# First rows' f32 products of the first two dense steps issued per tile of 128 rows, and a new table of places

## The chip, the core and the metric

The kernel runs on one core of one Trainium2 chip. The metric is device time in microseconds (us) of one execution, from the program's start to its end on that core; less is better.

## What is computed

Attention with a memory branch, and behind it a two-layer network on all 2304 rows:

```
scores = q @ k.T / 8, causal;  a = softmax(scores);  local = a @ v          # per batch and head, S=576, D=64
mem    = (phi(q) @ M_prev) / (phi(q) . z_prev + 1e-6)                        # phi(x) = elu(x) + 1
attn   = g * mem + (1 - g) * local                                           # g = sigmoid(beta) per head
x      = attn as [2304, 512]                                                 # 4 batches x 576 rows, 8 heads x 64
h      = x @ w_in                                                            # [512, 2048]
y      = (max(h, 0) + alpha * min(h, 0)) @ w_out                             # [2048, 512]
```

The two weights arrive as 64-bit floats; VectorE turns them into f32 with integer operations (three instructions for a piece of 128 rows).

## The kernel before

**Rows.** A batch has 576 rows: 64 first rows and four tiles of 128. The first 64 rows of the four batches make one group of 256 rows, called Z in the code (`gz`, batch number 4 in names), in two tiles of 128 rows, t = 0 and 1. Each other group has two tiles of 128 rows of one batch.

**First rows.** For each tile of Z the kernel turns q and k with TensorE (`tZ0`, `tZ1`), makes scores (`sZ0`, `sZ1`, PSUM tiles `s_0_69` and `s_0_68`, row maxima `zmx`), exponentials on ScalarE, and probabilities beside the memory branch's factors in the tiles `P_99` and `P_100` (`p4`, `oZ0`, `oZ1`). TensorE turns these and multiplies with the values; ScalarE writes the result in f32 to `x32` (`R` in the trace), 128 columns per tile. The scaling of the values needs their largest magnitude (`v4`), which needs the last of the loads of the first rows' v and M_prev.

**Dense steps.** The network goes in steps j = 0 to 7 of 256 of the 2048 hidden columns. For Z (and for the first group of batch 0) steps 0 to 3 are done in f32 straight from the converted weights `R`; step j of Z has phase name `h4_10j`. Before, such a step is two accumulation groups (f = 0, 1) of four matmuls with 256 moving columns, both tiles of rows at once, into one of two PSUM tiles (`h_126`, `h_125`); then ScalarE's relu into `r`, and two VectorE instructions into `gg`. Later steps use f16 halves of weights and rows, three matmuls where f32 has one. The second product (`y4_10j` and so on) accumulates in two PSUM tiles `y`, which are also used for turning.

**Order.** Nothing is scheduled while the program runs. Every instruction is recorded with a phase name; the table `PLACES` gives each instruction of each phase its place, and the program is written out in the order of these numbers. An engine runs its own instructions strictly in that order, so that one that waits holds up all behind it; DMAs are issued in that order too, almost all from SyncE's queue (SP in the trace).

```
places = {k: iter(map(int, x.split())) for k, x in PLACES.items()}
at = [next(places[op[7]]) for op in self.ops]
for i in sorted(range(len(at)), key=at.__getitem__):
```

**Fillers.** 40 f16 matmuls of `ones` (phases `N`, `n`) into `h_125` compute nothing that is used; they stand at the start of TensorE's order between the first rows' short pieces of work. Eight f32 matmuls `h_125<-R` (phases `n0` to `n3`) are fillers too.

**Names.** `C0x`, `D0x` and `C1x` are VectorE's conversions of the first half of the weights (outputs `R`), `C2x` and `C3x` those of the second half; `ast`, `oma` and `scd` come from alpha, which TensorE turns first (`bank<-ident,xn`); `bk0x` and `BK0x` turn q and k of batch 0, `s0..` are its scores, `P0..` its probabilities, `o0..` its values; `q1`, `bk1x` prepare batch 1. Nearly every instruction has line L1748, the line that writes out the recorded program, so tiles tell them apart.

Of the kernel before, what the change touches and what calls it, by code (L numbers as in the profile page):

```python
# [32 lines left out]
    "LZ0": (  # L33
        "28"
    ),
    "LZ1": (
        "35"
    ),
    "Lz": (
        "29 34 0"  # L40
    ),
    "LK0": (
        "89"
    ),
    "LK1": (
        "86"
    ),
    "LV0": (
        "96 95"
    ),  # L50
    "LV1": (
        "178 179"
    ),
    "I": (
        "1 7 2 8 9 31 10"
    ),
    "z": (
        "37 32 38 44 33 90"
    ),
    "N": (  # L60
        "6 11 12 13 14 15 16 17 18 19 20 21 22 23 24 25"
    ),
    "n": (
        "40 41 42 58 59 78 85 87 102 130 134 135 136 137 138 139 140 141 142 143 192 193 194 195"
    ),
    "J": (
        "43 49 50 51 175 39 53 54 55 56 61 64 69 70 72 75 80 77"
    ),
    "a4": (
        "66 98 100 116 117 167"  # L70
    ),
    "K": (
        "5 26"
    ),
    "tZ0": (
        "45 46 47 48 81 91 92 93 94 103 105"
    ),
    "sZ0": (
        "60 104 106 107 108 109 110 111 112 113 114 115 118 119 120 121 122 123 126 165 212 145 185 164 166 215 186"
    ),  # L80
    "tZ1": (
        "82 83 84 88 124 127 128 129 131 132 147"
    ),
    "sZ1": (
        "146 148 149 150 151 152 153 154 155 156 157 158 159 160 161 162 163 182 187 223 226 225 188 227 213 189 224"
    ),
    "v4": (
        "133 180 184 197 198 201 203 204 654 205"
    ),
    "p40": (  # L90
        "65 67 68 73 74"
    ),
    "p41": (
        "79 97 99 101 125"
    ),
    "p4": (
        "168 170 173 181 206 207 214 183 208 217 240"
    ),
    "oZ0": (
        "216 220 221 222 233 234 235 242 236 237 238 239 253 243 244 245 246 247 265 266 267 268 269 270 271 272 275 "  # L100
        "276 281 282"
    ),
    "oZ1": (
        "228 241 248 249 250 251 252 254 255 256 257 260 261 273 274 279 280 284 285 286 287 292 294 295 296 297 298 "
        "299 300 301"
    ),
    "LW00": (
        "27"
    ),
    "LW01": (  # L110
        "62"
    ),
    "LW02": (
        "171"
    ),
    "LW03": (
        "144"
    ),
    "LX00": (
        "288"  # L120
    ),
    "LX01": (
        "262"
    ),
    "LX02": (
        "283"
    ),
    "LX03": (
        "229"
    ),  # L130
    "C00": (
        "36 52 57"
    ),
    "n0": (
        "196 199"
    ),
    "C01": (
        "63 71 76"
    ),
    "n1": (  # L140
        "202 209"
    ),
    "C02": (
        "172 174 176"
    ),
    "n2": (
        "210 211"
    ),
    "C03": (
        "169 177 200"  # L150
    ),
    "n3": (
        "218 219"
    ),
    "D00": (
        "289 290 291"
    ),
    "c0": (
        "328 378 381 382 437 454 525 544 557"
    ),  # L160
    "D01": (
        "277 278 305"
    ),
    "D02": (
        "293 323 368"
    ),
    "D03": (
        "264 321 352"
    ),
    "LW10": (  # L170
        "401 402"
    ),
    "LW11": (
        "395 392"
# [5 lines left out]
        "439 429 466 450 467 468 474 506 529 700 655 656"  # L180
    ),
    "LW12": (
        "451 452"
    ),
    "C11": (
        "398 400 428"
    ),
    "LW13": (
        "446 445"
    ),  # L190
    "C12": (
        "453 455 456"
    ),
    "C13": (
        "447 448 449"
    ),
    "L0q": (
        "315 190 230"
    ),
    "L0k": (  # L200
        "336 332 338 30"
    ),
    "L0v": (
        "469 472 473 464"
    ),
    "a0": (
        "191 258 259 320"
    ),
    "bk00": (
        "306 307 308 309 310 302 303 304 311 329"  # L210
    ),
    "bk01": (
        "347 348 349 356 337 341 342 345 357 358 360 379 346 350 351 359"
    ),
    "v0": (
        "475 476 477 481 484 485 486 489 490 491 1161 492"
    ),
    "p00": (
        "263 313 314 322 366"
    ),  # L220
    "p01": (
        "231 232 312 317 318"
    ),
    "p0": (
        "367 375 383 420 493 494 495 384 496"
    ),
    "L0Q": (
        "316 385"
    ),
    "L0K": (  # L230
        "409 412"
    ),
    "L0V": (
        "509 482"
    ),
    "A0": (
        "319 431 503 520"
    ),
    "BK00": (
        "380 389 394 396 397 387 388 390 391 393"  # L240
    ),
    "BK01": (
        "410 413 416 417 421 411 414 415 418 427"
    ),
    "V0": (
        "510 512 524 580 581 597 612 715 613 679 682"
    ),
    "r02": (
        "425 426 460 540 555"
    ),  # L250
    "r03": (
        "386 399 488 533 554"
    ),
    "r0": (
        "638 647 699 713 714 716 717 712 719"
    ),
    "h4_100": (
        "324 325 326 327 330 331 333 334 335 362 363"
    ),
    "s011": (  # L260
        "440 458 457 459 470 465 500 501 497 498"
    ),
    "P010": (
        "502 504 514 513 532 519 515 526 547 550 551 556 558"
    ),
    "h4_101": (
        "339 340 343 344 353 354 355 361 376 403 377"
    ),
    "y4_100": (
        "434 441 435 442"  # L270
    ),
    "P011": (
        "499 521 517 531 537 527 565 566 567 568 570 571 574"
    ),
    "s013": (
        "507 518 522 534 535 539 528 536 523 553"
    ),
    "P012": (
        "541 542 543 562 589 561 575 588 590 593 594 599 604"
    ),  # L280
    "o011": (
        "601 602 603 621"
    ),
    "P013": (
        "577 578 546 582 538 579 607 608 609 610 622 625 626"
    ),
    "h4_102": (
        "364 365 369 370 371 372 373 374 438 461 462"
    ),
    "y4_101": (  # L290
        "436 443 471 444"
    ),
    "s015": (
        "559 560 563 572 587 591 573 592 576 595"
    ),
    "P014": (
        "614 615 516 616 545 624 627 634 635 636 637 644 645"
    ),
    "o013": (
        "658 659 660 664"  # L300
    ),
    "P015": (
        "628 630 661 631 548 642 663 665 666 667 668 674 675"
    ),
    "s017": (
        "620 639 632 641 652 650 640 653 633 651"
    ),
    "P016": (
        "681 683 606 684 662 691 685 692 693 694 704 705 707"
    ),  # L310
    "h4_103": (
        "404 405 406 407 408 419 423 424 463 479 480"
    ),
    "y4_102": (
        "478 549 487 552"
    ),
    "o015": (
        "676 677 678 697"
    ),
    "P017": (  # L320
        "686 695 605 696 689 706 708 709 710 711 722 723 724"
    ),
    "s031": (
        "738 740 742 739 757 759 761 758 771 766 765 805"
    ),
    "P030": (
        "772 784 781 780 836 878 806 820 1020"
    ),
    "o017": (
        "731 732 733 734"  # L330
    ),
    "bv00": (
        "741 1023 727 730"
    ),
    "bv01": (
        "767 1085 799 807"
    ),
    "bv02": (
        "830 1090 720 721"
    ),  # L340
    "bv03": (
        "810 811 745 796"
    ),
    "P031": (
        "822 842 846 850 847 876 874 875 877"
    ),
    "h0_100": (
        "671 702 718 743 746 747 748 749 752 754 756"
    ),
# [72 lines left out]
    "S22": (
        "839 867"
# [1328 lines left out]
def kernel(  # L1752
# [27 lines left out]
    Z = B  # L1780
    KD = DM // 128
# [57 lines left out]
    def raw(pos):  # L1839
        return R[pos]  # L1840
# [993 lines left out]
```

## Time and profile before

| | |
|---|---|
| three runs | 540.99, 539.5, 540.41 us; median 540.41 |
| profiled execution | 539.77 us, of which the span from first to last instruction is 538.0 |
| TensorE (PE) busy | 524.0 us, 97% of the span |
| VectorE (DVE) busy | 442.0 us, 82% |
| ScalarE (ACT) busy | 390.1 us, 73% |
| GpSimd (POOL) busy | 69.2 us, 13% |
| granted TensorE clock | 1.0 of full speed in every slice |

A busy TensorE is not a TensorE at its peak, since matmuls are pipelined and their ends are modelled; starts are what to go by. Idle time matters only on an engine that others wait for, so each stage has to be asked for itself.

### The profile page before, as it was taken

The page shows a single profiled execution, that of the slowest core. Times are in us where ns is not written, and L with a number is a line of the kernel's source. Part 1 is how long each engine was busy: PE and PEld are TensorE (multiplying, and loading weights), DVE is VectorE, ACT ScalarE, POOL GpSimd, SP SyncE. Part 2 cuts the span into 40 slices and gives each one's busy share as a digit, 9 for nine tenths or more (in the row PEclk, how much of TensorE's full clock was granted, in tenths as well). Part 3 has the DMA queues.
Part 4 walks back from the last instruction along what each step waited for, and adds up shares of the span by engine and source line. Part 5 has one row for each costly group of instructions (what it writes and reads, how often), then busy time and mean ns, then how long its engine had stood idle before and what let it go on. Part 6 is the DMA issues. An engine that isn't in the chain of part 4 may idle for free.

```text
span 538.0 us, 11935 instructions
## 1 busy us (share of the span) xinstructions
PE 524.0 (97%) x4419; PEld 352.6 (66%) x4419; DVE 442.0 (82%) x1167; ACT 390.1 (73%) x820; POOL 69.2 (13%) x142
## 2 busy tenths in 40 slices
PE   9999999999988999999999999999999999999996
PEld 4687456657564767576768666666766667666672
DVE  4999999999999999999987899988478867752321
ACT  4868998779987788988897796876376756842322
POOL 3000310302101021111112120111021110200000
PEclk9999999999999999999999999999999999999999
DMA  9999816669588799668999885659454643641101
GB/s 211 278 283 296 235 61 214 196 191 222 114 158 199 188 213 175 168 148 202 212 168 211 136 148 90 136 131 197 92 105 91 126 95 80 127 104 40 39 1 40
DMA packets 225586, 82.32 MB, mean 153 GB/s; under 512 B 216036, under 2 KB 216052, under 8 KB 225528
## 3 DMA queue, kind: packets, MB, share of 16 engines
q1 hardware_dynamic: 225344, 81.55, 66.4%
q8 instruction: 34, 0.56, 0.4%
q14 instruction: 24, 0.20, 0.1%
q10 hardware_dynamic: 184, 0.02, 0.0%
HBM read 35.15 MB, written 5.77 MB: 76 GB/s over the span
## 4 chain that ended last, share of the span: by engine, by line
PE 79%; DVE 14%; ACT 2%; DMA 2%; issue 1%; DVEq 0%; ACTq 0%
PE h L1748 33%; PE y L1748 32%; PE s L1748 7%; PE bank L1748 6%; DVE R L1748 5%; DMA PT<-P 2%; DVE P L1748 2%; DVE E L1748 2%; DVE q L1748 1%; PE s L1655 1%; DVE gg L1748 1%; DVE r L1748 1%; DVE t L1748 1%; ACT t L1748 1%; ACT R L1748 1%
## 5 line engine op out<-in xcount | busy, mean ns | idle before, releaser
L1748 PE MATMUL y<-R,gg 128*128 128x512 f16 (+1 forms) x832 | 233.6, 396 | 1.4 <-DVE t L1748 1.2
L1748 PE MATMUL h<-x,R 128*128 128x256 f16 x1536 | 214.8, 273 | 0.0
L1748 PEld LDWEIGHTS <-R 128*128 128x128 f16 x1536 | 144.3, 98 | 38.2 <-DVE r L1748 1.5
L1748 PEld LDWEIGHTS <-gg 128*128 128x128 f16 x768 | 72.8, 98 | 60.8 <-issue 2.3
L1748 POOL TENSOR_SCALAR E<-q,nrm,sm 128x64 f32<-128x64 f32 x112 | 56.6, 519 | 333.4 <-DVE sm L1748 246.4
L1748 ACT ACTIVATE E<-E,mx 128x320 f32<-128x320 f32 (+3 forms) x136 | 80.8, 599 | 14.4 <-DVE mx L1748 13.1
L1748 DVE SCALAR_TENSOR_TENSOR P<-E,mx,P 128x640 f16<-128x640 f32 (+3 forms) x112 | 75.8, 701 | 10.4 <-ACT P L1748 10.3
L1748 DVE SCALAR_TENSOR_TENSOR r<-r,oma,h 128x256 f32<-128x256 f32 x128 | 56.9, 472 | 26.3 <-ACT r L1748 26.0
L1748 ACT ACTIVATE P<-E,mx 128x512 f16<-128x512 f32 (+3 forms) x112 | 71.0, 673 | 7.5 <-POOL E L1748 6.2
L1748 PE MATMUL bank<-v,PT 128*128 128x64 f16 x1224 | 75.4, 193 | 1.0 <-DMA PT<-P 1.0
L1748 ACT ACTIVATE r<-h 128x512 f32<-128x512 f32 x72 | 41.8, 589 | 42.3 <-PE h L1748 34.6
L1748 PEld LDWEIGHTS <-PT 128*128 128x128 f16 x1224 | 60.3, 98 | 16.0 <-DMA PT<-P 2.4
L1748 DVE CUSTOM_DVE_ANT_0 E<-s,mask,pm 128x320 f32<-128x320 f32 (+3 forms) x96 | 56.8, 611 | 3.4 <-PE s L1748 2.4
L1748 ACT ACTIVATE gg<-r,gsc 128x512 f16<-128x512 f32 x56 | 39.7, 715 | 26.5 <-PE y L1748 20.1
L1748 DVE SCALAR_TENSOR_TENSOR gg<-r,gsc,gg 128x512 f16<-128x512 f32 x56 | 41.6, 748 | 17.6 <-ACT gg L1748 15.5
L1748 PE MATMUL s<-k,qT 128*128 128x512 f16 (+5 forms) x136 | 36.4, 290 | 1.8 <-DMA qT<-q 1.8
L1748 PE MATMUL s<-k,qS 128*128 128x192 f16 (+4 forms) x120 | 33.8, 294 | 1.2 <-DMA qS<-qT 1.2
L1748 PE MATMUL h<-R 128*128 128x256 f32 x144 | 34.7, 383 | 0.0
L1748 PEld LDWEIGHTS h<-R 128*128 128x128 f32 x144 | 26.1, 190 | 5.3 <-issue 1.7
L1748 ACT ACTIVATE xn<-bank,xsc 128x256 f16<-128x256 f32 x28 | 13.1, 468 | 19.8 <-PE bank L1748 19.7
L1748 ACT ACTIVATION_READ_ACCUMULATOR E<-E,mx 128x1 f32 x124 | 23.3, 188 | 0.0
L1748 ACT ACTIVATE R<-R,wsc 128x1024 f16<-128x1024 f32 x16 | 18.3, 1143 | 5.5 <-DVE R L1748 4.8
(186 smaller groups left out, 611.9 us busy)
## 6 DMA issues: line engine op xcount, KB each, us to landing
q<-in_q_dram SPq DMA_DIRECT2D x18, 256.0 KB, 4.2
vn<-in_v_dram SPq DMA_DIRECT2D x16, 256.0 KB, 4.6
out_dram<-t SPq DMA_DIRECT2D x16, 256.0 KB, 2.3
kn<-in_moe_w_in_dram SPq DMA_DIRECT2D x6, 512.0 KB, 6.0
kn<-in_moe_w_out_dram SPq DMA_DIRECT2D x6, 512.0 KB, 5.2
kn<-in_k_dram SPq DMA_DIRECT2D x12, 256.0 KB, 3.8
qS<-qT SPq DMA_DIRECT2D x24, 128.0 KB, 2.7
R<-in_moe_w_in_dram SPq DMA_DIRECT2D x4, 512.0 KB, 6.5
```

The costliest lines, as they stand in the source:

```text
L1655: first[1](*first[2], **first[3])
L1748: fn(*a, **kw)
```

## The change

Two things change: the code of the first two f32 steps of Z, and the whole table of places. In steps j = 0 and 1 of Z the loop over the two tiles of rows goes outermost: for each tile, each f, the four matmuls with 128 moving columns. That is 16 matmuls of 128 columns where 8 of 256 were, in each of the two steps, and the matmuls of the first tile no longer depend on the second tile's rows. The relu and the two VectorE instructions behind them are unchanged and still wait for all 16. Steps 2 and 3 are unchanged.

```diff
-        for f in range(2):
+        if f32 and g["id"][0] == str(Z) and j < 2:
+            for t in range(2):
+                for f in range(2):
+                    fc = 2 * j + f
+                    for kk in range(KD):
+                        T.matmul(hps[:, f, 128 * t:128 * t + 128], lhsT=raw(kk + 1)[:, fc * 128:fc * 128 + 128],
+                                 rhs=g["x32"][:, kk, 128 * t:128 * t + 128], start=(kk == 0), stop=(kk == KD - 1))
+        for f in range(2) if not (f32 and g["id"][0] == str(Z) and j < 2) else ():
...
     "h4_100": (
-        "324 325 326 327 330 331 333 334 335 362 363"
+        "309 310 311 350 351 355 356 357 358 359 363 365 366 367 368 369 389 418 405"
     ),
...
     "y3_313": (
-        "6213 6214 6215 6220 6221 6222 6216 6217 6218 6223 6224 6225 6219 6226 6230 6049 6228 6229"
+        "6229 6230 6231 6236 6237 6238 6232 6233 6234 6239 6240 6241 6235 6242 6246 6065 6244 6245"
     ),
```

What the new table does to the order is seen at three places.

**At the start.** On TensorE, just behind the two matmuls that spread z_prev (`y<-R`), a filler now stands ahead of the turn of alpha, and one more stands ahead of these matmuls:

```order
 L1748 MATMUL y_124<-R 128x512
 L1748 MATMUL y_123<-R 128x512
+L1748 LDWEIGHTS ones
+L1748 MATMUL h_125<-ones 128x512
 L1748 MATMUL bank_67<-ident,xn_103 128x16
```

So alpha's turn comes two fillers later. On VectorE, from its first conversion on, before:

```order
L1748 TENSOR_SCALAR R<-R 128x512
L1748 TENSOR_SCALAR igc<-igc 128x8
L1748 RECIPROCAL iom<-igc 128x8
L1748 TENSOR_SCALAR iom<-iom 128x8
L1748 SCALAR_TENSOR_TENSOR R<-R 128x512
L1748 TENSOR_SCALAR oma<-bank_67 128x16
L1748 TENSOR_REDUCE ast_89<-bank_67 128x1
L1748 TENSOR_SCALAR ast_89<-ast_89 128x1
L1748 SCALAR_TENSOR_TENSOR R<-R 128x512
L1748 TENSOR_REDUCE scd_87<-bank_67 1x1
```

and now:

```order
L1748 TENSOR_SCALAR R<-R 128x512
L1748 SCALAR_TENSOR_TENSOR R<-R 128x512
L1748 TENSOR_SCALAR igc<-igc 128x8
L1748 SCALAR_TENSOR_TENSOR R<-R 128x512
L1748 RECIPROCAL iom<-igc 128x8
L1748 TENSOR_REDUCE ast_89<-bank_67 128x1
L1748 TENSOR_SCALAR oma<-bank_67 128x16
L1748 TENSOR_SCALAR ast_89<-ast_89 128x1
L1748 TENSOR_SCALAR iom<-iom 128x8
L1748 TENSOR_REDUCE scd_87<-bank_67 1x1
L1748 TENSOR_SCALAR scd_87<-ident,scd_87 1x1
```

The third instruction of the first conversion (the second `SCALAR_TENSOR_TENSOR R<-R`) moved from behind alpha's two reductions to ahead of them.

**At the first dense step.** TensorE behind the first rows' values, before (`y<-ident,q_2` turns q of batch 0, `y<-ident,v_66` its k, which is kept in that buffer):

```order
L1748 MATMUL y_124<-ident,q_2_95 128x128 x3
L1748 MATMUL y_123<-ident,q_2_95 128x128 x4
L1748 MATMUL y_124<-ident,q_2_95 128x128
L1748 MATMUL h_126<-R 128x256 x8
L1748 MATMUL y_124<-ident,v_66 128x128
L1748 MATMUL h_125<-R 128x256 x2
```

and now:

```order
L1748 MATMUL y_124<-ident,q_2_95 128x128 x3
L1748 MATMUL h_126<-R 128x128 x3
L1748 MATMUL y_123<-ident,q_2_95 128x128
L1748 MATMUL h_125<-R 128x128 x4
L1748 MATMUL y_123<-ident,q_2_95 128x128
L1748 MATMUL h_125<-R 128x128
L1748 MATMUL y_123<-ident,q_2_95 128x128 x2
L1748 MATMUL y_124<-ident,q_2_95 128x128
L1748 MATMUL h_125<-R 128x128 x9
```

The first dense products stand five turns of q earlier, the two steps are mixed, and step 1 (`h_125`) is complete before step 0 (`h_126`).

**Where the change ends.** The last piece of VectorE's order that differs, at about 149 to 152 us of the run before (`P_100` are probabilities of batch 0's head 5, `xn_103` the rows that its heads 2 and 3 give, `k_0_101` the keys of batch 1):

```order
-L1748 SCALAR_TENSOR_TENSOR R<-R,wsc 128x1024
+L1748 RECIPROCAL mx_108<-sm_153 128x2
+L1748 SCALAR_TENSOR_TENSOR xn_103<-bank_67,xsc,xn_103 128x256
+L1748 SCALAR_TENSOR_TENSOR k_0_101<-kn_90,scr_127,k_0_101 128x10x64
+L1748 SCALAR_TENSOR_TENSOR q_0_93<-q_0_93,t_1_118 128x512
 L1748 SCALAR_TENSOR_TENSOR P_100<-E_0_92,mx_108,P_100 128x512
 L1748 SCALAR_TENSOR_TENSOR P_100<-E_0_92,mx_108,P_100 128x640
-L1748 SCALAR_TENSOR_TENSOR k_0_101<-kn_90,scr_127,k_0_101 128x10x64
-L1748 SCALAR_TENSOR_TENSOR q_0_93<-q_0_93,t_1_118 128x512
-L1748 SCALAR_TENSOR_TENSOR xn_103<-bank_67,xsc,xn_103 128x256
 L1748 ISA E_0_92,mx_107<-s_0_68,mask 128x448
```

The two `P_100` instructions moved behind three others; from the row `E_0_92,mx_107<-s_0_68` on, VectorE's order is the same in both kernels, and so is that of every other engine and of the DMA queue from about the same point on (their last differing rows lie at about 150 us too). All later places are 16 higher, the number of matmuls that were added.

Two more moves are of use below. On ScalarE the f16 copy of Z's rows (`x<-R`) stood behind the copies of batch 0's turned q and k; it now stands just behind the write of the first rows' results, ahead of the relu of step 1. In the DMA queue the third of the first weight pieces is issued ahead of the first rows' values, q and k of batch 0 in another order, and z_prev of batch 0 later.

## Rows read from the trace of the kernel before

**Rows 1.** Busy time by stage: stretch, its length, then each engine's.
```profile
5.60:13.50 7.90, 7.90 (x35) 3.88 (x34) 5.42 (x17) 4.69 (x11) 0.00 (x0) 1.00 1.11 243
13.50:28.00 14.50, 13.10 (x120) 8.74 (x118) 13.92 (x47) 12.26 (x47) 0.00 (x0) 1.00 0.98 283
28.00:60.00 32.00, 32.00 (x206) 23.46 (x205) 30.83 (x64) 25.96 (x53) 0.00 (x0) 1.00 0.99 278
60.00:100.00 40.00, 38.86 (x203) 23.93 (x203) 38.87 (x123) 36.24 (x94) 9.94 (x18) 1.00 0.49 153
100.00:157.00 57.00, 56.52 (x445) 36.37 (x444) 56.68 (x134) 49.29 (x83) 8.29 (x11) 1.00 0.76 180
157.00:176.00 19.00, 14.49 (x118) 8.13 (x115) 19.00 (x37) 14.11 (x25) 1.81 (x4) 1.00 0.86 199
176.00:533.50 357.50, 356.55 (x3304) 246.48 (x3300) 277.01 (x748) 245.10 (x511) 44.82 (x96) 1.00 0.62 128
```
**Rows 2.** Chain of waits, two pieces: start, duration, what.
```profile
171.39 3.94 DMA PT<-P
175.38 1.75 PE bank L1748 x54
```
**Rows 3.** Who waited for whom on TensorE, 157 to 180 us: total, times, longest.
```profile
PE s L1748 <- DMA qT<-q: 1.8, 1, 1.8
PE y L1748 <- DVE t L1748: 1.2, 1, 1.2
PE s L1748 <- DMA qS<-qT: 1.2, 1, 1.2
```
**Rows 4.** Timeline of VectorE: start, duration, what, idle time before it and releaser.
```profile
5.60 0.43 DVE L1748 TENSOR_SCALAR R<-R 128x512 int32<-128x512 int32 x1 [4.49 <-DMA R<-in_moe_w_in_dram]
...
9.05 0.17 DVE L1748 TENSOR_SCALAR oma<-bank 128x16 f32<-128x16 f32 x1 [1.79 <-PE bank L1748]
...
10.46 0.28 DVE L1748 TENSOR_REDUCE scd<-bank 1x1 f32<-1x128 f32 x1 [0.36 <-PE bank L1748]
...
12.13 0.68 DVE L1748 SCALAR_TENSOR_TENSOR R<-R 128x512 int32<-128x512 int32 x1
21.10 0.69 DVE L1748 TENSOR_REDUCE zmx<-s 128x8 f32<-128x512 f32 x1 [0.22 <-PE s L1748]
...
69.45 0.49 DVE L1748 CUSTOM_DVE_ANT_0 P<-s,mask 128x320 f32<-128x320 f32 x1 [0.33 <-PE s L1656]
```
**Rows 5.** Who VectorE waited for, 28 to 157 us.
```profile
DVE gg L1748 <- ACT r L1748: 0.5, 1, 0.5
DVE P L1748 <- PE s L1656: 0.3, 1, 0.3
DVE mw L1748 <- PE bank L1748: 0.3, 1, 0.3
```
**Rows 6.** Timeline of TensorE.
```profile
16.79 2.32 PE L1748 MATMUL h<-ones 128*128 128x512 f16 x10
18.95 1.02 PE L1748 MATMUL s<-mz,ident 128*128 128x512 f32 x2
...
27.84 0.56 PE L1748 MATMUL s<-PT,PT 128*64 128x64 f32 x10 [0.24 <-ACT PT L1748]
...
43.93 1.04 PE L1748 MATMUL y<-ident,q 128*128 128x128 f32 x8
44.81 2.32 PE L1748 MATMUL h<-R 128*128 128x256 f32 x10
46.97 1.04 PE L1748 MATMUL y<-ident,v 128*128 128x128 f32 x8
...
156.02 1.51 PE L1748 MATMUL bank<-v,PT 128*128 128x64 f16 x46
```
**Rows 7.** Weight loads by form: count, busy time, mean ns of one.
```profile
L1748 PEld LDWEIGHTS h<-R 128*128 128x128 f32 x144 | 26.1, 190 | 5.3 <-issue 1.7 <-ACT R L1748 0.4
```
**Rows 8.** Timeline of ScalarE.
```profile
48.41 1.05 ACT L1748 CAST x<-R 128x1024 f16<-128x1024 f32 x1
```

More of the change, by code (lines that the diff above doesn't have):

```diff
@@ L66 @@
[L66 to L86, printed above, removed]
@@ L107 @@
-    "LW00": (
-        "27"
-    ),
+        "30"
+    ),
+    "LZ1": (
+        "29"
+    ),
+    "Lz": (
+        "7 27 0"
+    ),
+    "LK0": (
+        "48"
+    ),
+    "LK1": (
+        "41"
+    ),
+    "LV0": (
+        "145 146"
+    ),
+    "LV1": (
+        "168 166"
+    ),
+    "I": (
+        "1 23 2 35 49 50 51"
+    ),
+    "z": (
+        "33 26 44 45 42 43"
+    ),
+    "N": (
+        "6 8 9 10 11 12 13 14 15 16 17 18 19 20 21 22"
+    ),
+    "n": (
+        "40 47 54 61 85 127 167 170 171 172 173 174 175 176 177 179 180 183 184 185 186 188 197 198"
+    ),
@@ new lines @@
+    "J": (
+        "32 37 39 63 66 52 55 53 56 60 64 65 68 69 70 72 123 164"
+    ),
+    "a4": (
+        "73 88 122 124 125 142"
+    ),
+    "K": (
+        "5 25"
+    ),
+    "tZ0": (
+        "57 58 59 62 77 84 86 87 90 92 93"
+    ),
+    "sZ0": (
+        "83 101 102 103 105 106 107 108 109 110 111 112 113 114 115 119 120 144 150 153 182 154 191 187 155 151 178"
+    ),
+    "tZ1": (
+        "78 80 81 82 98 94 95 96 97 116 128"
+    ),
+    "sZ1": (
+        "91 117 118 129 130 131 132 133 135 136 137 138 139 140 156 157 158 159 189 190 210 192 214 211 193 215 212"
+    ),
@@ new lines @@
+    "v4": (
+        "147 169 194 195 199 201 202 203 1106 204"
+    ),
+    "p40": (
+        "46 74 75 99 121"
+    ),
+    "p41": (
+        "79 89 104 134 141"
+    ),
+    "p4": (
+        "143 152 161 165 205 208 218 206 219 221 242"
+    ),
+    "oZ0": (
+        "220 222 223 226 227 228 229 230 231 232 233 234 235 238 239 240 241 256 257 258 259 260 271 272 276 277 279 "
+        "280 281 283"
+    ),
+    "oZ1": (
+        "237 243 244 245 246 247 248 249 251 252 253 254 255 261 273 274 275 278 282 284 285 286 287 288 289 290 297 "
+        "298 299 300"
+    ),
@@ L160 @@
     ),
     "D01": (
-        "277 278 305"
+        "339 340 342"
     ),
     "D02": (
-        "293 323 368"
+        "270 293 294"
     ),
     "D03": (
-        "264 321 352"
+        "264 265 268"
     ),
     "LW10": (
-        "401 402"
+        "423 429"
     ),
     "LW11": (
-        "395 392"
+        "458 457"
     ),
```

1039 lines of the change are left out of this document (495 added, 544 removed), and 96 rows, old and new, of tables.

## The prediction

> **What bounds the kernel now.** I read the table of stages first, to see which engine has no idle time where [rows 1]. (In its rows PE's busy time stands first, then weight loads, VectorE, ScalarE, GpSimd.) From 28 us to the end TensorE is busy for practically the whole stretch: 32.00 of 32.00, 38.86 of 40, 56.52 of 57, then 356.55 of 357.5. The exception is 157 to 176 us, with 14.49 of 19.00. There VectorE is busy for all 19.00, and from 100 us on its idle time is 0.32 us. So two engines are full until 176 us, and from there TensorE alone.
>
> Next I read the chain of waits where the one hands over to the other [rows 2]: `PT<-P`, a DMA that turns probabilities of VectorE, lands, and at 175.38 TensorE goes on from it. The list of who waited for whom on TensorE around that place [rows 3] has 1.8 us for qT, 1.2 for qS and 1.2 for VectorE's `t`: three waits, each for something that VectorE made, some through a DMA. A TensorE that comes to 157 us up to 1.8 us later than now only waits less there; one that comes earlier waits more. What decides the end is therefore when VectorE has done its work up to 176 us.
>
> The order is, as shown above, the same in both kernels, on every engine, from about 152 us on. So the change is worth what it shifts VectorE at that place, and nothing behind it can add or take. VectorE's order is filled with the same instructions up to there (the change adds matmuls alone), so its shift is the sum of the idle times that it loses or gains. Of these the trace lists few. In the first 28 us [rows 4]: 4.49 for the first weight piece, 1.79 for alpha's turn, 0.36 for the spread scale, 0.22 for the row maxima of the first scores. From 28 to 157 us [rows 5]: 0.5 for ScalarE's relu in front of `gg`, 0.3 in front of `mw`, 0.3 for scores in front of `P`. More than these, with breaks between instructions, the change can't give.
>
> **Parts of the change.**
>
> *Start, VectorE.* The first 4.49 us stay: the first load is still the first in the queue. The third conversion instruction, 0.68 us [rows 4], moves into the 1.79 us wait for alpha's turn. Alone that would be −0.68. But alpha's turn now stands two fillers later in TensorE's order; ten fillers took 16.79 to 18.95 us, so 0.216 each [rows 6], and TensorE goes from one to the next there: +0.43. Left is −0.25. Behind it come two short waits for TensorE (spread of `ast`, of `scd`), of which before showed 0.36; work of VectorE that covered them has moved ahead, so I give 0.2 to 0.25 back. Together 0 to −0.05; bounds −0.7 (fillers cost nothing) and +0.4 (they cost all, the moved instruction nothing).
>
> *First scores.* The 0.22 us wait for `zmx` [rows 4] closes if TensorE's scores of tile 0 come at least that much earlier against VectorE's work; by the order two fillers fewer stand directly ahead of them. −0.2; bounds −0.22 and +0.2.
>
> *The split.* Per step, 8 matmuls of 256 columns become 16 of 128. The trace shows two records, each with a weight load, for an f32 matmul: 144 [rows 7] for the 72 that read f32 weights (eight steps of 8, eight fillers). Ten records of 256 columns took 44.81 to 46.97, 0.216 each; eight of 128 columns, f32 on f32, took 43.93 to 44.81, 0.110 each [rows 6]. Two steps are 32 records of 0.216, 6.91, and become 64 of 0.110, 7.04: +0.13. From below, 64 of 0.108, exactly half: 0. From above, if each of the 64 had to wait for its own weight load at the mean of the group, 190 ns [rows 7]: 12.16 − 6.91 = +5.2. That mean belongs to loads that lie beside matmuls of 0.216, and the turns, which load new weights too, run at 0.110. I take the row that is the same operation in size and type, +0.13. It falls on TensorE at 32 to 47 us.
>
> The Trainium skill, page "TensorE: Matmul & The Clock Gate", section "Weight-path perf modes — Fast Weight Load (FWL) and DoubleRow", says that the fast load is not there for FP32 inputs, and its section "LDWEIGHTS (loading the stationary operand)" gives a load as columns over 1.2 ns, by which I estimate 107 ns for 128 columns. By this a load is as long as a pass of 128 columns, so the split would have no margin, and any load that is issued late would show. The trace agrees so far as the turns of 128 columns run at 0.110 with their loads beside them; by the page the sum stays as it is.
>
> *What the split releases.* The first dense product no longer waits for tile 1's rows. But TensorE has no idle time there to fill: its only wait around it is 0.24 us at 27.84 for a copy [rows 6], and 28 to 60 us is full [rows 1]. So the split lets products stand earlier than turns of q, it gives no TensorE time. What may gain is VectorE, which waits 0.5 us for the relu in front of `gg` [rows 5]: the step that is now complete first is so about where h was before, earlier than the one VectorE waited for. That wait closes, −0.4, and `mw`'s 0.3 perhaps too.
>
> *Where this goes.* At 69.45 us VectorE waits 0.33 for a score that TensorE makes [rows 4], TensorE being full from 28 us up to it [rows 1]. TensorE's work up to that score is the same, plus 0.13 of the split, so the score comes at the same time or 0.1 later, and what VectorE gained at 28 to 60 us it waits there: the 0.33 become about 1. Only the head's part could come through, if TensorE is early by it too; the fillers and turns up to 28 us have the same total, and TensorE's start hangs on the same loads, so TensorE is at most 0.24 early. Middle: 0, bounds −0.4 and +0.4.
>
> *Where it ends.* The two `P_100` instructions moved behind three others, so the turned probabilities land some 2 us later; such a DMA took 3.94 [rows 2]. What needs them are the values in the group of 46 matmuls at 156.02, in front of the wait of 1.8 us for qT [rows 3, 6]. A lateness of up to 1.8 us there takes the place of that wait. Free; if the cover were gone it would be 2 us less 1.8 on TensorE, still before VectorE decides. In return `xn_103` and `k_0_101` come 1 to 3 us earlier, for which TensorE has nothing idle.
>
> **The sum.** Head −0.05 − 0.2, split and middle +0.13 (the 0.13, which the score at 69.45 hands to VectorE), end 0: about −0.1. The profiled execution took 539.77, 0.64 under the median of the three runs, 540.41. So 539.7 for an execution like the profiled one and 540.3 against the median. About 0.3%, 1.6 us, is what a measurement of this kernel can tell from no change; the three runs alone spread over 1.5.
>
> **Rivals.**
>
> *B, VectorE's waits all close and nothing hands them back.* 0.7 at alpha's turn, 0.36, 0.22, 0.5, 0.3 and 0.33 are 2.4 in all [rows 4, 5]; with half of the rest of the idle time before 100 us, up to 3. For it: VectorE is the bound at 176, and a new order of the whole front touches each of them. Against: TensorE is full from 28 us and makes the scores at 69.45. It needs TensorE to come there early by as much, thus to lose work in front of it to places behind; the walk through the order shows some turns of q and k behind the dense steps, no more. −1.7 to −3: 537.4 to 538.7.
>
> *C, slower: ScalarE comes late.* The f16 copy of Z's rows, 1.05 us [rows 8], now stands ahead of the relu of the first finished step, on an engine with 25.96 of 32 us busy in 28 to 60 [rows 1]. If relu comes late, `gg` on VectorE waits more than its present 0.5, and squares of converted pieces that ScalarE makes come late behind it. From before's pace the latest of them would be 1.26 late if ScalarE had no slack; it has 6.04 us idle in the stretch, and the rival decides where less than 1.05 of that lies ahead of the relu. VectorE would lose 0.9 to 2.1 (the copy once, or at both places), and the wait at 69.45 gives back at most 0.33: 541 to 542.5.
>
> *D, slower: weight loads show.* The bound of the split, if loads of 128 columns don't hide: up to +5.2 on TensorE, at half of it +2.6. TensorE being full up to the score at 69.45, VectorE waits for all of it there. 542.5 to 545.5. Against: the turns at 0.110.
>
> *A, nothing that can be told.* The sum above, −0.9 to +0.9: 539.5 to 541.3.
>
> **How the numbers follow.** A 0.63, B 0.19, C 0.12, D 0.06. Faster than 538.8 is B and an edge of A: 0.20; slower than 542.0 is D, most of C's upper part and a little of A: 0.14; same 0.66. For the range of 8 in 10 I take A whole, two thirds of B and two thirds of C: 538.2 to 542.0.
>
> **What the profile after would show.** (1) At the start VectorE's wait for alpha's turn is spent partly on the conversion: about 1.4 to 1.6 us where it was 1.79, longer short waits behind it, no `zmx` wait. (2) The first dense matmuls of 128 columns begin at 31.5 to 32 us, at 0.108 to 0.115 each; 0.19 would be rival D. (3) The wait for the relu in front of `gg` is under 0.1; over 0.9 would be rival C. (4) The wait for scores near 69.5 is about 1, at the same time of day within 0.3; if the score comes over 1 us early, it is rival B. (5) From 100 us on VectorE is full, with 56.5 or more of 57, and TensorE's waits for qT, qS and `t` at 157 to 176 are there, changed by less than 0.5 beyond the shift. The prediction is wrong if VectorE's last common piece at 152 us stands more than 1.6 us from where it stood, or if two of the shifts that I give as zero have the same sign.

## The result, and the profile after

The changed kernel takes 543.08 us (median of 6 runs, 542.28 to 544.38) against 540.38 for the kernel before on the same chip: 1.0052 times as long, 95% interval 1.0037 to 1.0067. A second set of runs gave 543.37 and 1.0058 (1.0044 to 1.0072). So it is slower by 2 to 4 us, outside the range of the prediction. The profiled execution took 542.55, its span 540.7; that of before was 539.77 and 538.0, so the two profiles differ by 2.7 or 2.8, as the medians do. One execution, of e10 below, took 607.64 us at a mean granted clock of 0.849 and is left out of all medians and counts.

The table of stages of the kernel after, which answers to [rows 1] (stretch, its length, busy time of PE, weight loads, VectorE, ScalarE, GpSimd, then granted clock):

```profile
28.00:60.00 32.00, 32.00 (x239) 24.45 (x238) 30.92 (x67) 26.75 (x55) 0.00 (x0) 1.00 1.04 281
60.00:100.00 40.00, 38.73 (x202) 23.79 (x201) 37.78 (x120) 35.16 (x91) 8.91 (x18) 1.00 0.53 167
100.00:157.00 57.00, 56.31 (x421) 35.80 (x420) 55.54 (x131) 48.39 (x82) 12.12 (x11) 1.00 0.73 177
157.00:176.00 19.00, 13.42 (x117) 7.83 (x113) 19.00 (x38) 14.90 (x26) 1.80 (x4) 1.00 0.70 162
```

VectorE is busy for 37.78 of 40 us where it was 38.87, and from 100 to 157 us for 55.54 where it was 56.68. GpSimd, for its eleven instructions there, is busy 12.12 us where it was 8.29: the same instructions, longer. The list of who VectorE waited for, 28 to 157 us (answers to [rows 5]):

```profile
DVE P L1748 <- ACT P L1748: 1.0, 1, 1.0
DVE E L1748 <- PE s L1656: 0.7, 2, 0.4
DVE R L1748 <- DMA kn<-in_moe_w_in_dram: 0.5, 1, 0.5
DVE q L1748 <- PE y L1748: 0.4, 1, 0.4
DVE q L1748 <- ACT q L1748: 0.4, 1, 0.4
DVE gg L1748 <- PE y L1748: 0.4, 1, 0.4
DVE sm L1748 <- ACT P L1748: 0.3, 1, 0.3
```

The 1.0 and one of the 0.4 (ScalarE's q) stand at the end of the change, where the prediction gave nothing. VectorE's timeline there:

```profile
147.96 0.15 DVE L1748 SCALAR_TENSOR_TENSOR sm<-sm,C 128x2 f32<-128x2 f32 x1
148.03 1.26 DVE L1748 SCALAR_TENSOR_TENSOR R<-R,wsc 128x1024 f16<-128x1024 f32 x1
...
149.30 0.15 DVE L1748 RECIPROCAL mx<-sm 128x2 f32<-128x2 f32 x1
149.37 0.45 DVE L1748 SCALAR_TENSOR_TENSOR xn<-bank,xsc,xn 128x256 f16<-128x256 f32 x1
149.75 0.86 DVE L1748 SCALAR_TENSOR_TENSOR k<-kn,scr,k 128x640 f16<-128x640 f32 x1
150.55 0.67 DVE L1748 SCALAR_TENSOR_TENSOR q<-q,t 128x512 f32<-128x512 f32 x1
151.15 0.73 DVE L1748 SCALAR_TENSOR_TENSOR P<-E,mx,P 128x512 f16<-128x512 f32 x1
152.89 0.89 DVE L1748 SCALAR_TENSOR_TENSOR P<-E,mx,P 128x640 f16<-128x640 f32 x1 [1.00 <-ACT P L1748]
...
155.96 0.75 DVE L1748 SCALAR_TENSOR_TENSOR q<-q,scr,q 128x512 f16<-128x512 f32 x1 [0.38 <-ACT q L1748]
```

ScalarE's, and GpSimd's, of the same stretch:

```profile
149.60 0.72 ACT L1748 ACTIVATE P<-E,mx 128x512 f16<-128x512 f32 x1 [0.53 <-POOL E L1748]
152.02 0.83 ACT L1748 ACTIVATE P<-E,mx 128x640 f16<-128x640 f32 x1 [1.70 <-POOL E L1748]
```

```profile
148.28 3.71 POOL L1748 TENSOR_SCALAR E<-q,nrm,sm 128x64 f32<-128x64 f32 x2 [5.71 <-DVE sm L1748]
```

The chain reads backwards: VectorE's second `P` waits for ScalarE's, ScalarE's for GpSimd's `E`, and GpSimd's two instructions took 3.71 us together (1.29 and 2.44 less a small overlap). GpSimd waits for VectorE's sum (`sm`), which is at 147.96 here. In the kernel before the same pair is the row of POOL below, behind a sum at 145.89:

```profile
145.89 0.14 DVE L1748 SCALAR_TENSOR_TENSOR sm<-sm,C 128x2 f32<-128x2 f32 x1
146.13 1.24 POOL L1748 TENSOR_SCALAR E<-q,nrm,sm 128x64 f32<-128x64 f32 x2 [4.16 <-DVE sm L1748]
```

Two rows by which VectorE's lateness is read, before and then after: the first row of the order that is common again, and a reduction behind ScalarE's q.

```profile
152.06 0.60 DVE L1748 CUSTOM_DVE_ANT_0 E<-s,mask 128x448 f32<-128x448 f32 x1
154.53 0.67 DVE L1748 TENSOR_REDUCE nrm<-t 128x8 f32<-128x512 f32 x1
```

```profile
153.69 0.62 DVE L1748 CUSTOM_DVE_ANT_0 E<-s,mask 128x448 f32<-128x448 f32 x1
156.63 0.68 DVE L1748 TENSOR_REDUCE nrm<-t 128x8 f32<-128x512 f32 x1
```

Instruction by instruction, VectorE stands this much later than before: 0.19 at 27 us, 0.37 at 77, 0.65 at 138, 1.63 at 153.7, 2.10 at 156.6 and unchanged through 176. From there TensorE carries it to the end, and VectorE's rows are 2.2 late at 190 and 2.75 at 528; most of what is added are two longer waits of TensorE for `PT<-P` at 282 and 381 us, in a stretch whose order did not change.

### The profile page after: what moved, and what is told of

Read it like the earlier page. It is cut to its first block, busy times and chain, and to the rows that moved or that the text cites. A ratio compares the mean times of both kernels' runs of the same rounds, so it can differ in the third digit from the quotient of the medians.

```text
span 540.7 us, 11989 instructions
## 1 busy us (share of the span) xinstructions
PE 524.1 (97%) x4451; PEld 353.2 (65%) x4451; DVE 441.8 (82%) x1167; ACT 389.6 (72%) x820; POOL 71.8 (13%) x142
## 4 chain that ended last, share of the span: by engine, by line
PE 75%; DVE 12%; DMA 5%; ACT 4%; SPq 3%; issue 1%; POOL 1%; DVEq 0%; POOLq 0%
PE h L1748 31%; PE y L1748 30%; PE s L1748 6%; PE bank L1748 6%; DVE R L1748 4%; DMA PT<-P 3%; SPq L1748 3%; DVE E L1748 1%; DVE P L1748 1%; DMA q<-in_q_dram 1%; ACT E L1748 1%; DVE gg L1748 1%; ACT PT L1748 1%; ACT P L1748 1%; DMA kn<-in_moe_w_in_dram 1%
## 5 line engine op out<-in xcount | busy, mean ns | idle before, releaser
L1748 POOL TENSOR_SCALAR E<-q,nrm,sm 128x64 f32<-128x64 f32 x112 | 59.0, 539 | 346.6 <-DVE sm L1748 259.6
L1748 PE MATMUL bank<-v,PT 128*128 128x64 f16 x1224 | 73.4, 193 | 2.1 <-DMA PT<-P 2.1
L1748 PE MATMUL h<-R 128*128 128x256 f32 (+1 forms) x176 | 35.9, 344 | 0.0
L1748 PEld LDWEIGHTS h<-R 128*128 128x128 f32 x176 | 27.9, 191 | 4.4 <-issue 1.9
```

The costliest lines, as they stand in the source:

```text
L1748: fn(*a, **kw)
```

## The experiments

Each row is timed against the kernel before on the same chip; the last column is the median over its runs of TensorE's mean granted clock (before: 0.999 over 138 runs).

| run | median us | ratio to before, 95% interval | clock |
|---|---|---|---|
| after, first set | 543.08 | 1.0052, 1.0037 to 1.0067 | 0.9945 |
| e9, after again | 543.37 | 1.0058, 1.0044 to 1.0072 | 0.994 |
| e1, new front, old tail | 542.26 | 1.0028, 1.0009 to 1.0047 | 0.995 |
| e2, old front, new tail | 541.74 | 1.0029, 1.0016 to 1.0042 | 0.997 |
| e3, split alone | 540.72 | 1.0004, 0.999 to 1.0017 | 0.9975 |
| e4, new places, no split | 544.69 | 1.0084, 1.0061 to 1.0108 | 0.9945 |
| e6, e2 with sum back | 540.47 | 1.0003, 0.9992 to 1.0013 | 0.998 |
| e16, after with sum back | 541.74 | 1.0019, 1.0005 to 1.0033 | 0.9945 |
| e17, after, reduction beside | 542.46 | 1.0037, 1.0018 to 1.0056 | 0.9955 |
| e18, e2, reduction beside | 540.94 | 1.0014, 1.0004 to 1.0025 | 0.997 |
| e5, after, six fillers | 543.32 | 1.0062, 1.0041 to 1.0083 | 0.9955 |
| e7, e5 with sum back | 542.9 | 1.0051, 1.0033 to 1.0068 | 0.997 |
| e8, before, fillers later | 541.57 | 1.0027, 1.0016 to 1.0039 | 0.998 |
| e12, before, six fillers less | 540.59 | 1.0008, 0.9998 to 1.0019 | 0.999 |
| e10, old to 28 us, new to 142 | 541.75 | 1.0024, 1.0012 to 1.0036 | 0.996 |
| e11, old to 69 us, new to 142 | 540.81 | 1.0006, 0.9994 to 1.0019 | 0.998 |
| e13, before, two reductions later | 541.31 | 1.0009, 0.9995 to 1.0022 | 0.999 |
| e14, before, one reduction more | 541.68 | 1.0016, 1.0006 to 1.0026 | 0.999 |
| e15, before, three more | 542.31 | 1.0036, 1.0023 to 1.0048 | 0.9995 |

**The table in two halves.** At about 142 us every engine has done the same set of instructions in both kernels, so the table can be cut there: "front" is the order up to it, "tail" from it to 154 us. e1 has the new front and the old tail, e2 the old front and the new tail. VectorE's edit in e2 against before, shortened to its core:

```diff
-SCALAR_TENSOR_TENSOR sm_153<-sm_153,C_145 128x2
 SCALAR_TENSOR_TENSOR q_0_91<-q_0_93,scr_127,q_0_91 128x8x64
-RECIPROCAL mx_108<-sm_153 128x2
+ISA E_0_92,mx_109<-s_0_69,mask 128x576
+SCALAR_TENSOR_TENSOR sm_153<-sm_153,C_145 128x2
+SCALAR_TENSOR_TENSOR R<-R,wsc 128x1024
+RECIPROCAL mx_108<-sm_153 128x2
+SCALAR_TENSOR_TENSOR xn_103<-bank_67,xsc,xn_103 128x256
+SCALAR_TENSOR_TENSOR k_0_101<-kn_90,scr_127,k_0_101 128x10x64
+SCALAR_TENSOR_TENSOR q_0_93<-q_0_93,t_1_118 128x512
 SCALAR_TENSOR_TENSOR P_100<-E_0_92,mx_108,P_100 128x512
```

> The changed kernel with the order of before in one stretch only, that of VectorE's order from about 142 to 154 us (all engines and DMAs). Theory 'tail': of the 2.1 us that VectorE is late at 156 us, 1.4 come from two waits there (1.00 for ScalarE's P, 0.38 for ScalarE's q), behind a GpSimd instruction that took 2.44 us instead of 0.39; so the time falls by 1.2 to 1.6, to 541.3 to 542.0 against 543.1, the GpSimd instruction takes about 0.4 and neither wait shows. Rival 'front': the lateness grows in whatever order stands there because the front is late; then it stays at 542.6 to 543.5.

> The kernel before with the changed order in the stretch of 142 to 154 us alone. Theory 'tail': slower by 1.2 to 1.6 than before (541.6 to 542.0), with a wait of VectorE for ScalarE's P of 0.8 to 1.2 and a GpSimd instruction of over 2 us. Rival 'front': 540.0 to 540.8, as before.

Measured: e1 is 0.8 to 1.1 faster than the changed kernel by the medians and 1.3 to 1.6 by the ratios (the intervals overlap), and both waits are gone, but it is still 1.5 (ratio) to 2.0 (medians) over before; e2 alone is 1.5 over, with the same two waits (1.09 and 0.38). Both halves cost something; the tail's part came out as expected in the old front.

**The split.** e3 has two matmuls of 128 columns in each slot of one of 256, e4 the new table with unsplit matmuls, each in the place of its second half:

```diff
-MATMUL h_126<-R 128x256 x8
+MATMUL h_126<-R 128x128 x16
```

> The kernel before with the split alone: in the slot of each matmul of 256 columns two of 128, in the order of the changed code. Theory 'tail', with the prediction's price of the split (+0.13 on TensorE, half of which VectorE waits): 540.3 to 540.8. Rival 'split': weight loads of 128 columns show and the split itself makes the 2.7 us: 541.5 to 543.

> The new table with the unsplit matmuls of 256 columns, each in the place of its second half. Theory 'tail': the split has no part in the loss, 542.6 to 543.4, with the same waits of VectorE at about 152 and 156 us. Rival 'split': 540 to 541.5.

e3 can't be told from before. e4 missed: it was expected like the changed kernel and is slower by its median, with intervals that just overlap; in its profile VectorE waits 0.39 and 0.92 for the relu in front of `gg`, which the changed kernel doesn't. The split itself is not the loss.

**GpSimd.** e6 and e16 put only the sum and its reciprocal back, in the new tail and in the changed kernel; e17 and e18 leave them late and move a one-input reduction beside GpSimd's second instruction. VectorE's edits (in the first, rows of a few columns are left out):

```diff
+SCALAR_TENSOR_TENSOR sm_153<-sm_153,C_145 128x2
 SCALAR_TENSOR_TENSOR q_0_91<-q_0_93,scr_127,q_0_91 128x8x64
+RECIPROCAL mx_108<-sm_153 128x2
 ISA E_0_92,mx_109<-s_0_69,mask 128x576
-SCALAR_TENSOR_TENSOR sm_153<-sm_153,C_145 128x2
 SCALAR_TENSOR_TENSOR R<-R,wsc 128x1024
-RECIPROCAL mx_108<-sm_153 128x2
```

```diff
 SCALAR_TENSOR_TENSOR xn_103<-bank_67,xsc,xn_103 128x256
+TENSOR_REDUCE stq_85<-q_2_95 128x1
 SCALAR_TENSOR_TENSOR k_0_101<-kn_90,scr_127,k_0_101 128x10x64
```

> The second experiment (old front, new tail, 541.74) with two VectorE instructions of 0.15 us, the sum and the reciprocal that GpSimd waits for, back in front of the rows that they had been moved behind. Everything else of the new tail stays. Theory 'GpSimd': GpSimd starts 2 us earlier, beside other VectorE instructions, takes about 0.4 to 0.9 and neither ScalarE nor VectorE waits: 540.0 to 540.7. Rival 'rest of the tail': the loss sits in the later P, the order of DMAs or of TensorE there: 541.3 to 542.

> The changed kernel with only the sum and the reciprocal that GpSimd waits for put back ahead of the rows they had been moved behind. 'GpSimd' with 1.3 us of the loss: 541.6 to 542.2. If in the new front the lateness at 138 us and the clock make most of the loss: 542.3 to 543.

> The changed kernel with one VectorE reduction of batch 2's q (0.60, one input in SBUF) moved from 121 us to about 149.8 us, between the row of batch 0's heads 2 and 3 and the first two-input instruction beside which GpSimd's second instruction took 2.44. GpSimd starts no earlier. Theory 'two inputs': beside a reduction GpSimd gets through in about 0.4, the waits of 1.00 and 0.38 go, VectorE has 0.60 more in that place: 0.4 to 1.4 less than the changed kernel, 541.8 to 542.8. Rival 'late start': GpSimd is late because its order came late, whatever runs beside it; then it still takes over 2 us and the time is 543 to 544.

> The same move in the second experiment's kernel (old front, new tail, 1.3 us over before). Theory 'two inputs': GpSimd 0.4, no waits of VectorE at 150 to 156 us, 0.1 to 0.9 over before. Rival 'late start': GpSimd over 2 us, the waits stay, 1.5 to 2.1 over before.

GpSimd's row in e2, e6 and e18, each from its own timeline:

```profile
148.07 3.80 POOL L1748 TENSOR_SCALAR E<-q,nrm,sm 128x64 f32<-128x64 f32 x2 [5.65 <-DVE sm L1748]
```

```profile
146.26 1.21 POOL L1748 TENSOR_SCALAR E<-q,nrm,sm 128x64 f32<-128x64 f32 x2 [4.17 <-DVE sm L1748]
```

```profile
147.76 1.66 POOL L1748 TENSOR_SCALAR E<-q,nrm,sm 128x64 f32<-128x64 f32 x2 [5.66 <-DVE sm L1748]
```

With two instructions of 0.15 us back (e6) the loss of the new tail is gone, to 0.2 of 1.6, and the changed kernel gets back two thirds of its loss (e16); in both the intervals of the pair do not overlap. With the late start kept and a reduction beside it (e18), the pair takes 1.66 instead of 3.80, no wait of VectorE is left at 140 to 160 us, and the time falls by half of the loss although VectorE has 0.6 more to do there; e17's median falls as expected too. The intervals of e18 and e2 overlap, as do those of e17 and the changed kernel, so the times alone don't show this; the rows do. A late start is not enough for the price: it takes the instructions beside GpSimd. Even those are not enough in every execution. In e5 (below) VectorE, ScalarE and GpSimd have the order of the changed kernel, the sum is as late, the same instructions run beside GpSimd, and still the second of the pair took 0.39 and VectorE does not wait at 140 to 160 us:

```profile
148.61 1.66 POOL L1748 TENSOR_SCALAR E<-q,nrm,sm 128x64 f32<-128x64 f32 x2 [6.04 <-ACT q L1748]
```

Of five profiles with that order and no reduction in it (after, e2, e4, e5, e9) four have the long instruction, 2.44 to 2.52.

**Fillers.** e5 adds six fillers to TensorE's waits at 10.5 to 15.4 us, e7 does so with the sum back; e8 moves six of before's fillers from 9 to 13 us to 17 us, e12 leaves them out (its edit):

```diff
-WARM = 16, 24
+WARM = 16, 18
```

> The changed kernel with six more filler matmuls, two in each of three waits of TensorE at 10.5 to 15.4 us (0.36, 0.41 and 0.40 in the profile after), where before had fillers. Theory 'clock': in some executions the granted clock falls to 1.2 GHz behind these waits, as it did at 11 to 14 us in the first experiment's profile, and TensorE comes late to the scores; with the waits filled the clock stays up at 10 to 15 us and the time falls by 0.5 to 1.2 from the changed kernel's 543.1, to 541.9 to 542.6. Rival 'order': the front loses by its order of work and loads alone, and six fillers change nothing or cost up to 0.5: 542.8 to 543.6.

> The changed kernel with both repairs, the six fillers and the two VectorE instructions back. If both theories hold and are all of it: 540.2 to 541.2. If a part of the front's loss has another cause, it stays between 541.2 and 542.

> The kernel before with six of TensorE's fillers moved from 9 to 13 us to 17 us, so that TensorE waits there; nothing else is moved. Theory 'clock': the granted clock falls in some executions near 10 to 15 us (mean granted clock of a run 0.993 to 0.998, where before has 0.998 to 1.0), and the median is 0.3 to 1.2 later. Rival 'order': the waits alone cost nothing and the runs stay at 539.8 to 540.6 with the clock of before.

> The kernel before without six of its fillers at 9 to 13 us (in an earlier experiment they were moved to 17 us, where they pushed the second scores back by 1.4). TensorE then waits there and nothing else changes. Theory 'clock': the granted clock falls behind these waits in some executions, the runs' mean granted clock is 0.993 to 0.998 and the median 0.3 to 1.2 later than before, 540.6 to 541.5. Rival: waits at 9 to 13 us cost nothing, 539.9 to 540.5.

e5 and e7 missed: no gain. e7 is even slower than e16, which has the same tail without the fillers; the profile of e7 (541.21, its fastest run) does not show why, and this stays open. In e5's profile GpSimd's price is missing, and a late load that costs VectorE 1.2 (below) stands in its place. e8 does not test the clock: its fillers at 17 us push the second scores back, and VectorE waits 1.38 for `zmx`. e12 does: TensorE is busy 2.35 and 2.00 of 3.00 us at 9 to 12 and 12 to 15 us, the runs' clock stays at 0.999, and the loss is 0.4 (−0.1 to 1.0). Thinner fillers alone do not bring the lower clock; a cost of up to 1.0 is not excluded.

**Which part of the front.** e10 and e11 have the split, the old tail, the old order up to VectorE's 28 us or 69 us, and the new one from there to 142 us. At the cut of e11, VectorE's order against e3:

```diff
 ISA P_100,mx_108<-s_0_69,mask 128x320
+SCALAR_TENSOR_TENSOR nrm_106<-nrm_106,igc 128x16
 ISA E_0_92,mx_109<-s_0_69,mask 128x320
+TENSOR_TENSOR kap<-wsc 128x1
```

> The changed kernel once more, for a second profile and more runs beside the kernel before. 542.6 to 543.5. Theory 'two parts': VectorE's two waits at 152 and 156 us (GpSimd) are some 1.3 of it, the rest is the front. If GpSimd's instruction of 2.44 us is a matter of chance, as one profile with the same order (0.39 us) makes it, the waits may be missing here, and the time is then 1.0 to 1.4 less.

> With the split, the old tail and the old order up to 28 us of VectorE, from there to 142 us the new order. The new front as a whole cost 2.0 us (first experiment, 542.26 against 540.23), the split alone 0.2 to 0.5 (third). Theory 'loads': the loss is made at 60 to 90 us, by VectorE's waits for scores at 77 us and for a weight piece at 84.6 us; then it stays here: 541.3 to 542.4. Rival 'start': it is made by the thinner fillers and later loads of the first 28 us; then 540.2 to 541.1.

> The same with the old order up to VectorE's scores at 69 us and the new one from there to 142 us. Theory 'loads': most of the loss is still here, 541.0 to 542.2, with the wait for the weight piece at 84 us. Rival 'start', or a loss in the dense steps at 28 to 69 us: 540.2 to 541.0.

e9, the changed kernel again, has the same waits of 1.00 and 0.38. By the ratios 28 to 69 us costs 1.0 (e10 less e11), 69 to 142 no more than can be told (e11 less e3), the start 0.2, or 0.6 by the medians (e1 less e10); the intervals of e10 and e11 just overlap, those of e1 and e10 widely. The two profiles don't show the 1.0: VectorE is 0.33 late at 156 us in e10 and 0.51 in e11.

**Lateness.** e13 moves two reductions out of VectorE's full stretch, e14 and e15 repeat one and three; the edit of e14:

```diff
-        for i in range(i0, i1) if b not in (Z,) else ():
+        for i in (i for i in range(i0, i1) for _ in range((1, 2)[i] if b == 2 and i < 2 else 1)) if b not in (Z,) else ():
```

> The kernel before with two VectorE reductions of batch 2's q (0.60 each, at 121 and 126 us) moved to about 209 us, where their result is used; all other engines as before. If the end follows VectorE's state at 156 to 176 us one to one, 1.2 less: 538.9 to 539.4 against 540.3, with TensorE's waits at 157 to 170 shorter. Rival: TensorE, ScalarE or a DMA decides there as soon as VectorE is earlier: 539.7 to 540.4.

> The kernel before with the first of these reductions done twice (one VectorE instruction of 0.60 us more at 121.7 us, with the same result). It makes VectorE as late at 138 us as the changed kernel's front does (0.65). Theory 'lateness': 0.6 more, 540.7 to 541.2, and a mean granted clock as before (0.999). Theory 'lateness and clock': TensorE's longer waits at 157 to 170 us make the granted clock fall in more executions, 541.3 to 542.0 with clocks of 0.992 to 0.998, as in the changed kernel.

> The same with three more of these instructions, 1.8 us of VectorE. Theory 'lateness': 541.9 to 542.4. Theory 'lateness and clock': 542.6 to 543.8, with mean clocks of 0.992 to 0.998.

0.6 us more on VectorE cost 0.9 (0.3 to 1.4) and 1.8 cost 1.9 (1.2 to 2.6): one to one, without a lower clock. 1.2 us less gave nothing: VectorE then waits 0.8 for ScalarE's `r`, 0.3 for TensorE and 0.2 for ScalarE's `R` between 100 and 157 us. So the order before stands on an edge, as far as these two reductions test it: later costs in full, earlier is worth nothing. No version here beats the kernel before.

## Why the prediction was wrong

**The step that failed is "Where it ends".** It followed the two moved `P_100` instructions forward, to the DMA and TensorE, found the cover of 1.8 us there, and priced the move at nothing. It did not follow the other rows of the same move backward. The sum that GpSimd waits for had moved too, ahead of the piece of the order that it looked at, and so had its reciprocal, which stands in that piece. The chain of GpSimd, ScalarE and VectorE that starts at the sum was never named, though the prediction's own rule says that VectorE's shift at about 152 us decides. There VectorE stood 1.63 late, just past the 1.6 that the prediction gives as a sign that it is wrong. Measured: 1.00 + 0.38 at VectorE in the profile, 1.4 by e2 against e6, 1.8 by the changed kernel against e16 (2.8 less 1.0). Nor does it hold that nothing behind that place can add or take: VectorE's lateness went from 2.10 to 2.75 in the profile after, and from 2.06 to 5.57 in e9.

**"Middle: 0" failed too, by less.** The score at 69.45 was taken as the place where VectorE's gains and losses of 28 to 60 us are levelled, and nothing was priced from there to 152 us. VectorE has no idle time there in [rows 5], and that was read as if none could arise. After the change it waits 0.38 for scores at 76.70 (no wait before, 0.17 or less in the profiles of the old order) and 0.48 for the weight piece at 84.57. The rows:

```profile
70.00 0.49 DVE L1748 CUSTOM_DVE_ANT_0 E<-s,mask 128x320 f32<-128x320 f32 x1 [0.28 <-PE s L1656]
76.70 0.49 DVE L1748 CUSTOM_DVE_ANT_0 E<-s,mask 128x320 f32<-128x320 f32 x1 [0.38 <-PE s L1656]
84.57 0.69 DVE L1748 TENSOR_SCALAR R<-kn 128x1024 int32<-128x1024 int32 x1 [0.48 <-DMA kn<-in_moe_w_in_dram]
```

The lateness grows from 0.19 at 27 us to 0.37 at 77 and 0.65 at 138, so by 0.46 where the bound was 0.4, and e14 shows that such a lateness counts in full. But these two waits are not shown to be the loss: e11's profile has both (0.34 and 0.44), and e11 can't be told from before. By the runs most of the loss of the middle lies at 28 to 69 us, where e10's profile does not show it. The scores at 69.45 themselves came 0.55 later (70.00 for 69.45), not 0 to 0.1, and VectorE waited 0.28 for it, not about 1.

**The start** was put at −0.25 and came out at +0.19 at 27 us: the first weight piece landed 0.9 later (6.50 for 5.60), the wait for alpha's turn was 1.18, the one for `zmx` closed as said, and 0.37 for the load of q took its place.

```profile
6.50 0.43 DVE L1748 TENSOR_SCALAR R<-R 128x512 int32<-128x512 int32 x1 [5.39 <-DMA R<-in_moe_w_in_dram]
```

The prediction left this first wait as it was, since the load is still the first in the queue. It is, issued at 0.73 us in both. Yet the work on it begins at 6.23 to 6.86 in all seven profiles that have the new start and the split, at 5.26 to 6.15 in the twelve with the old start, and at 5.57 in e4. No run shows why.

**The split** was sized nearly rightly: TensorE's rows after, three of the dense products and the turns behind them,

```profile
31.89 0.83 PE L1748 MATMUL h<-R 128*128 128x128 f32 x6
...
34.22 2.17 PE L1748 MATMUL h<-R 128*128 128x128 f32 x18
36.23 0.27 PE L1748 MATMUL y<-ident,v 128*128 128x128 f32 x1
...
37.01 1.73 PE L1748 MATMUL h<-R 128*128 128x128 f32 x14
38.57 0.38 PE L1748 MATMUL y<-ident,v 128*128 128x128 f32 x2
```

begin at 31.89 as forecast, and 18 records take 2.01 us (34.22 to 36.23), 0.112 each: 64 of them 7.15, +0.24 where +0.13 was said. Rival D is out. The relu's wait in front of `gg` closed as forecast, so rival C, which had the right sign, had the wrong place.

**What is left.** Of 2.8 to 3.1 us, 1.4 to 1.8 are GpSimd's. A part of the 1.0 that e16 still loses is VectorE's lateness from the front: at about 140 us it is 0.62 to 1.12 in the eight profiles of the whole new front, and −0.57 to 0.62 in the six with the old front and no reduction moved or added. Beside that the runs show a lower clock and a late load, but not what brings them. All 12 runs of the changed kernel have mean granted clocks of 0.992 to 0.998; over the 332 runs of all kernels, each against its own mean, 0.001 less goes with 0.21 us more, so 0.0045 less with about 1.0. That is a correlation, no experiment. e16's profile shows where, in stretches of 3 us:

```profile
9.00:12.00 3.00, 2.15 (x13) 1.68 (x13) 2.38 (x13) 3.00 (x7) 0.00 (x0) 0.84 1.26 261
12.00:15.00 3.00, 3.00 (x10) 1.60 (x9) 3.00 (x8) 0.84 (x4) 0.00 (x0) 0.59 1.10 263
165.00:168.00 3.00, 1.30 (x7) 0.58 (x7) 3.00 (x9) 3.00 (x6) 1.63 (x4) 1.00 0.72 159
168.00:171.00 3.00, 3.00 (x10) 1.32 (x9) 2.99 (x5) 1.26 (x3) 0.00 (x0) 0.51 1.40 210
```

TensorE had waited (2.15 and 1.30 busy of 3.00), and then ran at the lower of its two levels, 1.2 GHz, for most of a stretch (0.59 and 0.51 of full speed). The first of these made VectorE wait 1.00 for `zmx`. Behind the second, a dense matmul starts at 173.57 where the profile after has it at 173.22, although VectorE's `q` row in front of it was 1.16 earlier (154.80 for 155.96). About 1.0 of these 1.5 comes back within 4 us, because TensorE in the profile after waits there for VectorE and for `PT<-P`; what is left of the 1.16 at 177 us is 0.61, so about 0.5 is lost. The rows of e16, then of after:

```profile
173.57 0.27 PE L1748 MATMUL h<-x,R 128*128 128x256 f16 x1
177.14 1.74 PE L1748 MATMUL bank<-v,PT 128*128 128x64 f16 x54
```

```profile
173.22 0.28 PE L1748 MATMUL h<-x,R 128*128 128x256 f16 x1
177.75 1.75 PE L1748 MATMUL bank<-v,PT 128*128 128x64 f16 x54 [0.44 <-DMA PT<-P]
```

In the profile after TensorE waited about as long at both places and the clock stayed at 1.00, as it did in e15 behind a wait at 162 to 168 us (3.69 busy of 6.00). The rows of after:

```profile
9.00:12.00 3.00, 2.22 (x13) 1.26 (x12) 1.70 (x11) 2.82 (x7) 0.00 (x0) 1.00 1.21 274
165.00:168.00 3.00, 0.94 (x9) 0.66 (x7) 3.00 (x9) 2.26 (x5) 1.80 (x4) 1.00 0.77 204
```

The late load is the second `t<-part`, in four profiles of the whole new front (e1, e5, e9, e17; 4.0 to 4.9 us to landing, 2.4 to 2.9 in the other profiles). The third of these loads is as late (4.2 to 4.8) in nine profiles, before's among them, where VectorE does not wait for it. VectorE's row in e9:

```profile
172.12 0.75 DVE L1748 SCALAR_TENSOR_TENSOR t<-y,u,t 128x512 f32<-128x512 f32 x1 [2.04 <-DMA t<-part]
```

Why these come with the new front more than with the old one is not settled.

## What to carry to other kernels

When an instruction is moved, follow also what its small companions release: a sum of 0.15 us can be the start of a chain over two other engines that ends at the engine that sets the time. An engine without idle time in the profile of before is not one that can't wait after; price a reorder at every place where it depends on another engine, not only where it waits now. One profile is one execution: the wait that is about half of the loss is missing in one of five. And before a reorder is judged by what it saves on the full engine, make that engine later and earlier by a known amount: here the first cost one to one and the second gave nothing.

## What the runs showed of the hardware

GpSimd's `E<-q,nrm,sm` (128x64, f32) is slowed by some of VectorE's instructions, and by when they start. In the profile after, from 95 us on, 81 of these instructions had no VectorE instruction with two large tensor inputs, both in SBUF, beside them for over 0.1 us and took 0.39 to 0.42; the 31 that had took 0.83 in the median and up to 2.64. Of these 31, eight took only 0.39 to 0.40, and they had begun 0.10 to 0.21 us ahead of VectorE's instruction. Of the 23 slower ones 22 had begun behind it, or less than 0.02 ahead. The one left is that of this case: it began at 149.55, beside `xn`, 0.20 ahead of `k<-kn,scr,k` at 149.75, and still ended only at 151.99, after VectorE's row of instructions was done (151.88). In e5 it began 0.19 ahead of the same instruction and took 0.39. What decides between the two is not known; spans on GpSimd are rough.

Reductions, and instructions with one of their inputs in PSUM (`r<-r,oma,h`, `E<-s,mask`, `xn<-bank,xsc,xn`), did not slow it. But a single input is not always harmless: in the profile of before the integer instruction `R<-kn` (96.20 us, 0.70 long, one input) began 0.05 behind a GpSimd instruction, with no two-input instruction beside it, and that one took 0.94; so it did in all ten profiles with this order (0.93 to 0.94). VectorE itself loses little: `k<-kn,scr,k` took 0.86 beside GpSimd and 0.87 in the kernel before, and behind the eight that began first its instructions took up to 0.11 longer (`q<-q,t` 0.80 at 342.9, 0.69 otherwise).

The Trainium skill, page "SBUF — State Buffer", section "Who interferes with whom", has it that a VectorE instruction with two SBUF inputs contends with a GpSimd instruction that reads SBUF, and that one with at most one does not, outside VectorE's two-port modes. The trace agrees on the two inputs (up to 2.64 against 0.42 at most); in which mode `R<-kn` ran no run here shows. Of the two-port modes it also says that whichever issues first gets the port pair for its whole instruction. The trace has the same pattern for two inputs, in 30 of the 31, and differs in the one at 149.55.
